# Small transfers on eight DMA engines, and the first output sums moved ahead of the last weight chunk

## The chip, the core and the metric

The kernel runs on one NeuronCore of a Trainium2 chip. The core has a matrix engine (PE, with its weight load PEld), a vector engine (DVE), a scalar engine (ACT), GpSimd (POOL) and a sync engine (SP). Sixteen DMA engines move data between the device memory (HBM) and the on-chip memory; in this kernel POOL issues the loads of inputs and weights, and SP issues constants, small copies and the output. The metric is the device time of one execution in microseconds, lower is better.

## The reference

Two stages run one after the other. The first is causal attention with a bias made from a running sum, for 8 batches, 8 heads, 576 tokens and 64 features per head. The second is a spectral mix over the result `x` of shape (8, 576, 512): the first 64 frequencies along the tokens are each multiplied by a complex 512 x 512 matrix of their own, transformed back, and the sum goes through one more product.

```python
# attention, per batch and head
cum = np.cumsum(np.maximum(s, 0.0), axis=-1)
scores = scale * (q @ k.T) + np.minimum(-(cum[:, None] - cum[None, :]), 0.0)   # causal
x = softmax(scores) @ v                       # heads side by side: (B, S, 512)
# spectral mix
X = np.fft.rfft(x, axis=1)[:, :64]
Y = zeros; Y[:, m] = X[:, m] @ (w_r[m] + 1j * w_i[m])       # 64 modes
y = np.fft.irfft(Y, n=S, axis=1)
u = x + y
out = u + np.maximum(u @ w_ch, 0.0)
```

The inputs `w_r` and `w_i` are 64 x 512 x 512 floats each, 134 MB together, and are by far the largest thing that is read.

## The kernel before

**Attention and forward transform.** A step `n` of 32 handles two heads of one batch: group `g` (four of them, 128 of the 512 features each) and batch `b`. POOL loads q, k and v. `transposes` turns q and k into `qt` and `kt`, `scores` forms the exponentials, `av` the weighted sums, which go to `x_all`; `fft` multiplies them with the transform matrix `Ff_sb` into `xs`. The row of running sums that the bias needs is row 64 of `qt`. For the first two steps `cum_rows` copies it from the on-chip tile `ncum_sb`. That tile is also stored once to device memory, `ncum_dram` (L586), and for the 30 later steps `cum_rows` loads two rows of it (L342), one for each head.

**Weights.** The 64 modes are cut into 8 chunks of 8 (`c`, `NCK` = 8). For each group, chunk and real or imaginary part the weights are one unit of 1 MB as bf16, read as float32 and converted on the way. POOL issues a unit as two transfers (the last one as four), in the order group, chunk, real, imaginary. `modes(g, c)` multiplies a chunk: 16 products in four groups of four, the first two groups with the real part, the last two with the imaginary part. A dictionary `meanwhile` can put other work ahead of one of the four groups (L486 to L494). Groups 0 to 2 add their products to `y_acc`; the last group (`g` = 3) gives, with `y_acc`, the finished `y_sb` of the chunk.

**Back transform and output.** The output has 4608 rows, made as 18 pairs of 128 rows (`pairs`). For pair `i`, `us[i]` is x plus the back transform of Y, and `zs[i]` is the same times `w_ch`. The back transform is a product of `G_sb` (128 rows, 16 for each chunk: 8 modes, real and imaginary) with `yv`. The tile `yv` holds the chunks' rows on its partitions, once as Y (`which` = 0) and once as Y times `w_ch` (`which` = 1). A chunk's 128 result rows (modes by batches) become 16 partitions by 8 batches by copies on chip: for the early chunks in `gather`, from chunk 4 on partly with a transfer on SP's queue, `spread` (L511 to L513): chunks 4 and 5 send `which` = 1, chunks 6 and 7 send both.

For the first two pairs the sums over chunks 6 and 7 do not wait for `spread`. `add_last` multiplies the chunk's result, as it stands, with a sparse copy of the matrix, `Gx_sb` (and `Gt_sb` for the 64 left-over tokens). These are loaded from the constants `d_Gx` and `d_Gt` (L634, L638). `add_y` with rows up to `GK` = 96 covers chunks 0 to 5.

The order around the end is written out by hand (L862 to L918): chunks 0 to 5, then chunk 6 with its transposes (`y_transposed`) and its product with `w_ch` (`y_times_wch`), then chunk 7 with two pieces of other work put inside. Ahead of chunk 7's third group stands `first_z` for both pairs: the z sums over chunks 0 to 5 (12 products for `add_y` and `add_last` together), and ahead of the fourth group `first_u`: x itself (`add_x`), the u sums over chunks 0 to 5, and chunk 6's share. After chunk 7 the last transposes, its product with `w_ch`, and a list of steps for all pairs, given as a string (L953), lead to the 20 output transfers on SP's queue.

**Constants.** `G_sb` is loaded from `d_G` with 128 rows (L280). Each DMA engine works off its share of a transfer as packets, one for each contiguous row, and ends it with a small packet that raises a semaphore.

Of the kernel before, what the change touches and what calls it, by code (L numbers as in the profile page):

```python
# [11 lines left out]
BF16 = mybir.dt.bfloat16  # L12
# [6 lines left out]
def kernel(  # L19
# [11 lines left out]
    nc = tc.nc  # L31
    B, H, S, D = q.shape
# [6 lines left out]
    NPAIR = B * H  # L39
    NG = DM // P  # L40
# [5 lines left out]
    MC = 8  # L46
    NCK = NM // MC
# [12 lines left out]
    HP = P // 2  # L60
# [25 lines left out]
        np.concatenate([negm_np, negm4_np], axis=1).astype(np.float32), name="c_negm"  # L86
    ).ap()
    d_Ff = nc.inline_tensor(Ff_np, name="c_Ffwd").ap()
    d_G = nc.inline_tensor(G_np, name="c_Ginv").ap()

    NX = 2
    Gx_np = np.stack([G_np[2 * MC * c :, : NF * P][: 2 * MC] for c in range(NCK - NX, NCK)], axis=1)
    d_Gx = nc.inline_tensor(np.ascontiguousarray(Gx_np), name="c_Ginvx").ap()
    Gt_np = np.stack([G_np[2 * MC * c :, NF * P : S][: 2 * MC] for c in range(NCK - NX, NCK)], axis=1)
    d_Gt = nc.inline_tensor(np.ascontiguousarray(Gt_np), name="c_Ginvt").ap()

    ctx.enter_context(tc.manual_schedule())
    gp = ctx.enter_context(tc.tile_pool(name="globals", bufs=1))
# [15 lines left out]
    auxpool = aux.enter_context(tc.tile_pool(name="aux_psum", bufs=2, space=PSUM, side="right"))  # L114

    dpool = ctx.enter_context(tc.tile_pool(name="dram", bufs=1, space=bass.MemoryType.DRAM))
    ncum_dram = dpool.tile([NPAIR, S + HP], BF16, name="ncum_dram")
    at = ExitStack()
    ap_ = at.enter_context(tc.tile_pool(name="attn", bufs=1))
    qkpool = at.enter_context(tc.tile_pool(name="qk_sb", bufs=2))  # L120
# [215 lines left out]
    def cum_rows(n):  # L336
        if n >= N:
            return
        g, b = divmod(n, B)
        p0 = b * H + 2 * g  # L340
        if n >= 2:
            nc.sync.dma_start(out=qt[n % NQ][D : D + 1, :, :], in_=ncum_dram[p0 : p0 + 2, :S].unsqueeze(0))  # L342
            return
        for h in range(2):
            nc.sync.dma_start(out=qt[n % NQ][D : D + 1, h, :], in_=ncum_sb[p0 + h : p0 + h + 1, :])
# [124 lines left out]
    def modes(g, c, meanwhile=None):  # L470


        ps = auxpool.tile([P, DM], FP32, name="yp", tag="aux")
        cols = xs[g % 2].rearrange("p q k h r b m -> p q k (h r b) m")

        def product(ri, q_, cg):
            k0 = HP if ri == 1 and c == 0 and cg == 0 else 0
            nc.tensor.matmul(  # L478
                ps[32 * cg : 32 * cg + 32, :],
                cols[k0:, q_, 1 - ri, :, c * MC // 2 + cg],  # L480
                wt[(g, c, ri)][cg // 2][k0:, 2 * (cg % 2) + q_, :],
                start=(ri == 0 and q_ == 0), stop=(ri == 1 and q_ == 1),
                tile_position=(k0, 32 * cg), skip_group_check=True,
            )

        for x in range(4):  # L486
            ri, y = divmod(x, 2)
            if meanwhile and x in meanwhile:
                meanwhile[x]()
            for z in range(4):  # L490
                if meanwhile:
                    product(ri, z // 2, 2 * y + z % 2)
                else:
                    product(ri, y, z)  # L494
        if g == 0:
            nc.vector.tensor_copy(out=y_acc[:, c, :], in_=ps)
        elif g < NG - 1:
            nc.vector.tensor_tensor(out=y_acc[:, c, :], in0=ps, in1=y_acc[:, c, :], op=ALU.add)  # L498
        else:
            yb = spool.tile([P, DM], FP16, name="y_sb", tag="y")  # L500
            for cols in halves if c == NCK - 1 else [slice(0, DM)]:
                nc.vector.tensor_tensor(
                    out=yb[:, cols], in0=ps[:, cols], in1=y_acc[:, c, cols], op=ALU.add
                )
            if c >= NCK - 2:
                spread(c, 0, yb)
            return yb
# [2 lines left out]

    def spread(c, which, rows):  # L511

        nc.sync.dma_start(out=yv[16 * c : 16 * c + 16, :, which, :], in_=rows)  # L513

# [65 lines left out]
    with tc.tile_pool(name="sc_psum", bufs=2, space=PSUM) as scpool, \  # L582
            tc.tile_pool(name="tr_psum", bufs=1, space=PSUM) as trpool, \
            tc.tile_pool(name="av_psum", bufs=1, space=PSUM) as avpool:
        cum_rows(0)
        nc.sync.dma_start(out=ncum_dram[:, :S], in_=ncum_sb)  # L586
        transposes(0, 0)
        transposes(0, 1)
        load(loads_qk(2) + loads_v(2))
        pad_p()  # L590
        for n in range(N):
            if n in (0, 2):
                nc.vector.memset(xs_flat[n // 2].bitcast(FP32), 0.0)
            tails_due = loads_tails(n // B + 1)[n % B - 3 : n % B - 2] if 2 < n % B < 5 else []
            load((loads_qk(n + LA) if n % 2 else []) + loads_v(n + LA) + tails_due, loads_w(on_chip[n]))
            if n == N // 2 + 1:
                nc.gpsimd.dma_start(out=wch_sb, in_=moe_w_ch.rearrange("(dt p) e -> p dt e", p=P))
            cum_rows(n + 1)
            scores(n, 0)
            av(n - 1, 1)  # L600
            if n and n % B == 0:
                scores(n, 1)
                fft(n - 1)
                av(n, 0)
                mode_products(n, 0)
                transposes(n + 1, 0)
                mode_products(n, 1)
                transposes(n + 1, 1)
                continue
            mode_products(n)  # L610
            transposes(n + 1, 0)
            scores(n, 1)
            i = first_pairs[n - N + len(first_pairs)] if n >= N - len(first_pairs) else None
            if i is not None:
                first_transposed(i, 0)
            transposes(n + 1, 1)
            fft(n - 1)
            av(n, 0)
            if i is not None:
                first_product(i, 0)  # L620
                first_transposed(i, 1)
            if i is not None:
                first_product(i, 1)
        av(N - 1, 1)
        fft(N - 1)
# [72 lines left out]
    def y_transposed(yb, c=NCK):  # L698
        ps = auxpool.tile([P, DT, P], FP16, name="yt_ps", tag="aux")
        for dt in range(DT):  # L700
            nc.tensor.transpose(ps[:, dt, :], yb[:, bass.ts(dt, P)], ident16h)
        yt = yt_first[:, :, c % NY, :] if c < NCK - 2 else spool.tile([P, DT, P], FP16, name="yt_sb", tag="yt")
        nc.scalar.copy(out=yt, in_=ps)
        return yt
# [104 lines left out]
    def u_of(i):  # L809
        return [us[i][:, x, :] for x in range(2)]  # L810
# [48 lines left out]
    def z_of(i):  # L859
        return [zs[i, x] for x in range(2)]  # L860
# [20 lines left out]
    assert not order_z and not ahead  # L881
    c = NCK - 2
    yb6 = modes(NG - 1, c)
    yt = y_transposed(yb6)
    vb6 = y_times_wch(c, yt)


    def first_u():
        add_x(0)
        add_y(u_of(0), 0, 0, slice(0, GK))  # L890
        add_last(u_of(0), 0, yb6, c=0)

    def first_z(i):
        add_y(z_of(i), i, 1, slice(0, GK))
        add_last(z_of(i), i, vb6, c=0)

    yb = modes(NG - 1, NCK - 1, {2: lambda: (first_z(0), first_z(1)), 3: first_u})

    yt = spool.tile([P, DT, P], FP16, name="yt_sb", tag="yt")
    for x in range(2):  # L900
# [95 lines left out]
```

## Time and profile before

| what | value |
|---|---|
| median of 3 runs | 441.92 us (440.32 to 442.31) |
| the profiled execution's own time | 442.11 us |
| its span, first to last instruction | 440.3 us |
| mean granted PE clock | 0.925 |
| busy: PE, DVE, ACT, POOL | 340.8, 252.5, 226.0, 171.7 us |
| read from HBM, written | 163.58 MB, 9.51 MB |
| share of the chain that ended last: DMA, PE, DVE | 53%, 25%, 15% |
| chunk 7's first products start | 399.35 us |
| chunk 7's last group of products starts | 406.48 us |
| first output transfer is issued | 411.97 us |

The chain of waits is made by going back from the last instruction, at each step to what released it. The span is what the profiler saw between the first and the last instruction; the time of a run includes some 1.8 us around it. Times inside the kernel are counted from the start of the span. The clock column of a window is the share of full speed that PE was granted: a product of 512 columns takes 0.22 us at full and 0.43 us at half clock.

### The profile page before, as it was taken

To read this page: it belongs to the slowest core of one execution; us is meant where nothing else is said; L and a number is where in the kernel's file an instruction comes from. 1 tells how busy PE (TensorE), PEld (TensorE's weight loads), DVE (VectorE), ACT (ScalarE), POOL (GpSimd) and SP (SyncE) were. 2 spreads that over 40 slices of the span, in tenths; PEclk is the share of its full clock that TensorE was granted. 3 is DMA by queue.
4 is the path that set the end of the run, shared out by engine and by line. 5 is a ranking of instruction groups with operands and counts; after the bars stand their busy time and mean duration, and the time that the engine had idled before them with its cause. 6 is when DMAs were issued, how large, how long until landed. Compare 5 with 4: busy or idle time off the path is not lost.

```text
span 440.3 us, 10592 instructions
## 1 busy us (share of the span) xinstructions
PE 340.8 (77%) x4409; PEld 203.7 (46%) x4409; DVE 252.5 (57%) x574; ACT 226.0 (51%) x421; POOL 171.7 (39%) x257
## 2 busy tenths in 40 slices
PE   1588999899695977973939458899987797778995
PEld 1365666465463644641616125556554345432341
DVE  7667776677573555752715315766655344450795
ACT  1387878267463634860727024766651334330794
POOL 6555454424353444323444343433322212310293
PEclk9999999999988888995968767999999989996999
DMA  9999999999999999999999999999999999996498
GB/s 179 207 206 206 204 206 208 207 209 207 207 205 207 210 207 210 207 209 208 205 209 208 209 208 209 207 210 206 210 211 212 212 211 211 203 218 121 155 381 347
DMA packets 69063, 93.30 MB, mean 212 GB/s; under 512 B 25932, under 2 KB 27592, under 8 KB 69016
## 3 DMA queue, kind: packets, MB, share of 16 engines
q0 software_dynamic: 61424, 81.28, 104.6%
q1 hardware_dynamic: 7592, 11.36, 7.2%
q8 instruction: 34, 0.56, 0.5%
q14 instruction: 13, 0.11, 0.1%
HBM read 163.58 MB, written 9.51 MB: 393 GB/s over the span
## 4 chain that ended last, share of the span: by engine, by line
DMA 53%; PE 25%; DVE 15%; issue 3%; POOL 2%; ACT 1%; DVEq 0%; POOLq 0%
DMA w_sb<-in_moe_w_i_dram 21%; DMA w_sb<-in_moe_w_r_dram 17%; DMA qk<-in_k_dram 8%; DMA qk<-in_q_dram 5%; PE sc_ps L397 3%; DVE xs L468 3%; DVE qt L359 3%; PE z_ps L681 3%; PE yp L478 3%; DVE x_all L443 2%; PE av_ps L433 2%; PE sc_ps L391 2%; PE tr_ps L355 2%; DVE xt L553 2%; PE z_ps L773 2%
## 5 line engine op out<-in xcount | busy, mean ns | idle before, releaser
L405 ACT ACTIVATE p_sb<-sc_ps,cumt_sb 128x576 f16<-128x576 f32 (+1 forms) x256 | 141.9, 636 | 21.8 <-PE sc_ps L397 21.4
L397 PE MATMUL sc_ps<-qt,kt 128*128 128x512 bf16 (+2 forms) x384 | 76.8, 312 | 6.9 <-ACT kt L359 6.1
L243 POOL DMA_DIRECT2D v<-in_v_dram x72 | 51.4, 714 | 60.6 <-DMA w_sb<-in_moe_w_i_dram 12.8
L243 POOL DMA_DIRECT2D w_sb<-in_moe_w_i_dram x62 | 38.5, 623 | 89.2 <-DMA w_sb<-in_moe_w_i_dram 28.3
L359 DVE COPY qt<-tr_ps 64x576 bf16<-64x576 bf16 x64 | 47.8, 747 | 41.5 <-PE tr_ps L355 41.5
L478 PE MATMUL yp<-w_sb,xs 128*32 128x512 bf16 (+1 forms) x480 | 42.2, 431 | 29.1 <-DMA w_sb<-in_moe_w_i_dram 25.4
L355 PE MATMUL tr_ps<-ident,qk 64*64 64x64 bf16 x1152 | 34.3, 205 | 33.8 <-DMA qk<-in_k_dram 16.0
L243 POOL DMA_DIRECT2D w_sb<-in_moe_w_r_dram x60 | 37.4, 624 | 53.0 <-DMA w_sb<-in_moe_w_r_dram 33.3
L397 PEld LDWEIGHTS <-kt 128*128 128x128 bf16 x384 | 38.3, 105 | 34.5 <-ACT kt L359 12.8
L391 PE MATMUL sc_ps<-negm,ident 128*128 128x256 bf16 x256 | 53.5, 293 | 0.1
L355 PEld LDWEIGHTS <-qk 64*64 64x64 bf16 x1152 | 26.4, 117 | 51.7 <-DVE kt L359 20.3
L376 ACT ACTIVATE p<-sc_ps,cumt 128x64 f16<-128x64 f32 x32 | 10.1, 314 | 73.8 <-PE sc_ps L372 73.6
L433 PE MATMUL av_ps<-v,p_sb 128*128 128x65 f16 x1024 | 44.2, 197 | 1.8 <-DVE x_all L443 0.6
L359 ACT COPY kt<-tr_ps 64x576 bf16<-64x576 bf16 x32 | 22.8, 714 | 40.8 <-DVE qt L359 40.1
L433 PEld LDWEIGHTS <-p_sb 128*128 128x128 f16 x1024 | 37.4, 100 | 9.6 <-DVE x_all L443 5.4
L468 DVE CAST xs<-ft_ps 64x128 bf16<-64x128 f32 x128 | 36.7, 287 | 7.3 <-PE ft_ps L458 5.7
L478 PEld LDWEIGHTS <-xs 128*32 128x32 bf16 (+1 forms) x512 | 17.8, 146 | 46.0 <-DMA w_sb<-in_moe_w_i_dram 24.6
L438 DVE TENSOR_REDUCE den<-av_ps 128x5 f32<-128x10 f32 x64 | 10.8, 169 | 48.3 <-PE av_ps L433 47.3
L443 DVE TENSOR_TENSOR x_all<-av_ps,rcp 128x320 f16<-128x320 f32 x64 | 31.5, 492 | 2.2
L498 DVE TENSOR_TENSOR y_acc<-yp,y_acc 128x512 f32<-128x512 f32 x16 | 11.1, 692 | 29.2 <-PE yp L478 28.5
L539 ACT COPY z<-z_ps 128x512 f32<-128x512 f32 x22 | 12.9, 586 | 26.9 <-PE z_ps L571 14.2
L458 PE MATMUL ft_ps<-Ff_sb,x_all 128*64 128x192 f16 (+1 forms) x320 | 24.4, 266 | 1.0 <-DVE x_all L443 1.0
(107 smaller groups left out, 439.4 us busy)
## 6 DMA issues: line engine op xcount, KB each, us to landing
w_sb<-in_moe_w_r_dram POOLq DMA_DIRECT2D x60, 512.0 KB, 13.6
w_sb<-in_moe_w_i_dram POOLq DMA_DIRECT2D x55, 512.0 KB, 13.2
out_dram<-r_w SPq DMA_DIRECT2D x16, 512.0 KB
v<-in_v_dram POOLq DMA_DIRECT2D x72, 64.0 KB, 11.1
qk<-in_q_dram POOLq DMA_DIRECT2D x15, 288.0 KB, 12.0
qk<-in_k_dram POOLq DMA_DIRECT2D x15, 288.0 KB, 13.2
x_all<-in_moe_w_r_dram POOLq DMA_DIRECT2D x4, 512.0 KB, 8.4
w_sb<-in_moe_w_i_dram POOLq DMA_DIRECT2D x3, 384.0 KB, 12.7
```

Source lines behind the costliest of these rows:

```text
L243: nc.gpsimd.dma_start(out=dst, in_=src)
L355: nc.tensor.transpose(ps[rows, r, :], src[rows, r, :], ident16[rows, rows])
L359: copy(out=to[:, :, :, half * RH : half * RH + RH], in_=ps[HP * i : HP * i + HP].rearrange("d r (h p) -> d h p r", h=2),)
L391: nc.tensor.matmul(ps[:, bass.ds(w * S, W)], ident16, negm[:, bass.ts(r, W)], start=True, stop=False, skip_group_check=True,)
L397: nc.tensor.matmul(ps[:, c0 : c0 + i1 - i0], keys[:, w, r, :], qh[:, i0:i1], start=False, stop=True, skip_group_check=True,)
L405: nc.scalar.activation(out=pt[:, poff[x] : poff[x] + S - w * W], in_=ps[:, w * S : (w + 1) * S - w * W], func=ACTF.Exp, bias=cumt_sb[:, x, ...
L433: nc.tensor.matmul(ps[:, I, r : r + NCH], lhsT, rhs, start=(i == 0), stop=(i == len(todo) - 1), skip_group_check=True,)
L443: nc.vector.tensor_tensor(out=x_all[:, g, b, :, D * h : D * h + D], in0=ps[:, :, 1 : NCH], in1=rcp.unsqueeze(2).to_broadcast([P, NT, D]), ...
L458: nc.tensor.matmul(ps[HP * q_ : HP * q_ + HP].rearrange("p h f -> p (h f)"), x_all[:nT, g, b, T, q_::2], Ff_sb[:nT, T, :], start=(T == 0), ...
L468: nc.vector.tensor_copy(out=xs[g % 2][HP * h : HP * h + HP, q_, :, h, :, b, :], in_=a)
L478: nc.tensor.matmul(ps[32 * cg : 32 * cg + 32, :], cols[k0:, q_, 1 - ri, :, c * MC // 2 + cg], wt[(g, c, ri)][cg // 2][k0:, 2 * (cg % 2) + ...
L681: nc.tensor.matmul(zs[i, x], xts[i][:, x, dt, :], wch_sb[:, dt, :], start=(dt == 0), stop=(last and dt == DT - 1), skip_group_check=True,)
```

## The change

The change has two parts. It has no effect on what is computed.

The first part lays out small transfers on SP's queue so that the outermost dimension of one side has eight entries. The constants `G_sb`, `Gx_sb` and `Gt_sb` are read from an array of eight blocks with an unused row behind each. The running sums are stored in pieces of 144 values, with 16 unused values between, and a step's two rows are read as eight pieces of 288 bytes where before there were two of 1152. `spread` sends a chunk's 16 rows as two transfers of eight rows; chunk 7 keeps one transfer of 16.

The second part moves work of the first two pairs. `add_x`, the u sums over chunks 0 to 5 and chunk 6's u share go from inside chunk 7 to around chunk 6's transposes. The z sums over chunks 0 to 5 go to behind chunk 6's product with `w_ch`, ahead of all of chunk 7's products. Chunk 6's z share (`add_last` with `vb6`) stays ahead of chunk 7's third group.

```diff
+    def eighths(a, name):
+        n = len(a) // 8
+        t = np.zeros((8, n + 1) + a.shape[1:], a.dtype)
+        t[:, :n] = a.reshape((8, n) + a.shape[1:])
+        return nc.inline_tensor(t, name=name).ap()[:, :n]
-    d_G = nc.inline_tensor(G_np, name="c_Ginv").ap()
+    d_G = eighths(G_np, "c_Ginv")
-    d_Gx = nc.inline_tensor(np.ascontiguousarray(Gx_np), name="c_Ginvx").ap()
+    d_Gx = eighths(Gx_np, "c_Ginvx")
-    d_Gt = nc.inline_tensor(np.ascontiguousarray(Gt_np), name="c_Ginvt").ap()
+    d_Gt = eighths(Gt_np, "c_Ginvt")
...
-    ncum_dram = dpool.tile([NPAIR, S + HP], BF16, name="ncum_dram")
+    NE8 = 8
+    CP = 2 * S // NE8
+    ncum_dram = dpool.tile([NPAIR, S // CP, CP + 16], BF16, name="ncum_dram")
...
-            nc.sync.dma_start(out=qt[n % NQ][D : D + 1, :, :], in_=ncum_dram[p0 : p0 + 2, :S].unsqueeze(0))
+            nc.sync.dma_start(
+                out=qt[n % NQ][D : D + 1, :, :],
+                in_=ncum_dram[p0 : p0 + 2, :, :CP].rearrange("h x t -> (h x) t"),
+            )
...
     def spread(c, which, rows):
-        nc.sync.dma_start(out=yv[16 * c : 16 * c + 16, :, which, :], in_=rows)
+        n = 2 * MC if c == NCK - 1 else NE8
+        for r in range(0, 2 * MC, n):
+            nc.sync.dma_start(
+                out=yv[2 * MC * c + r : 2 * MC * c + r + n, :, which, :], in_=rows[B * r : B * (r + n), :]
+            )
...
-        nc.sync.dma_start(out=ncum_dram[:, :S], in_=ncum_sb)
+        nc.sync.dma_start(
+            out=ncum_dram[:, :, :CP], in_=ncum_sb.rearrange("c (x t) -> c x t", t=CP)
+        )
...
     yb6 = modes(NG - 1, c)
+    add_x(0)
     yt = y_transposed(yb6)
+    add_y(u_of(0), 0, 0, slice(0, GK))
+    add_last(u_of(0), 0, yb6, c=0)
     vb6 = y_times_wch(c, yt)
-
-    def first_u():
-        add_x(0)
-        add_y(u_of(0), 0, 0, slice(0, GK))
-        add_last(u_of(0), 0, yb6, c=0)
+    add_y(z_of(0), 0, 1, slice(0, GK))
+    add_y(z_of(1), 1, 1, slice(0, GK))
     def first_z(i):
-        add_y(z_of(i), i, 1, slice(0, GK))
         add_last(z_of(i), i, vb6, c=0)
-    yb = modes(NG - 1, NCK - 1, {2: lambda: (first_z(0), first_z(1)), 3: first_u})
+    yb = modes(NG - 1, NCK - 1, {2: lambda: (first_z(0), first_z(1))})
```

## The prediction

> **What bounds the kernel now.** I read the slices first, then the chain of waits from 335 us on, then the clock by stretches, last the transfers and their completion marks. The slices show DMA busy at nine tenths or more up to slice 36 at a steady 203 to 218 GB/s after the first slice: until about 405 us the weight stream sets the pace. The chain says how that hands over to the tail (columns: start, length, what):
>
> ```profile
> 335.86 16.85 DMA w_sb<-in_moe_w_i_dram
> ...
> 352.75 0.66 PE yp L478 x7
> ...
> 381.76 0.45 POOL w_sb L243
> ...
> 383.57 15.64 DMA w_sb<-in_moe_w_r_dram
> ...
> 399.35 1.09 PE yp L478 x6
> 400.44 0.96 PE z_ps L773 x2
> 401.41 0.85 PE z_ps L784 x2
> 402.26 0.99 PE z_ps L773 x3
> 403.25 0.85 PE z_ps L784 x3
> 404.11 1.00 PE yp L478 x4
> 405.11 0.57 PE u_ps L803 x2
> 405.68 0.43 PE u_ps L773 x2
> 406.12 0.43 PE u_ps L784 x2
> 406.55 0.60 PE yp L478 x4
> ```
>
> A weight load that lands at 352.71 starts chunk 3's products; from there PE work leads to the issue of the last loads at 381.76; chunk 7's real weights land at 399.21. From 399.35 the chain is PE alone: two groups of products, the sums of the first two pairs (L773, L784), a group, the u sums, the last group. By the timeline that group starts at 406.48. Its weights were there at 405.13 (below), so PE is 1.35 us late. Everything after it (33.9 us: last transposes, 18 result pairs, 9.4 MB out) hangs on that start, and the output queue is full from 419.6 on (402 GB/s), so I shift the tail one to one.
>
> Why PE is late shows in the windows (from:to, length, PE busy, PEld, DVE, ACT, POOL, granted clock, DMA share, GB/s), cut at the steps in which the clock changes in this trace, 3.41 us:
>
> ```profile
> 394.91:398.33 3.42, 1.43 (x8) 0.53 (x8) 1.09 (x2) 0.59 (x1) 0.00 (x0) 1.00 1.12 215
> 398.33:401.74 3.41, 2.39 (x12) 0.68 (x12) 0.00 (x0) 0.00 (x0) 0.00 (x0) 0.50 1.01 201
> 401.74:405.15 3.41, 3.41 (x15) 0.85 (x14) 0.00 (x0) 0.00 (x0) 0.00 (x0) 0.50 0.32 67
> 405.15:408.57 3.42, 2.85 (x17) 1.07 (x17) 0.76 (x2) 0.59 (x2) 0.00 (x0) 1.00 0.00 0
> ```
>
> A window with PE busy for 1.43 us is followed by half clock; a full window restores it. In the other such steps 1.50 us or less was followed by half clock and 1.85 or more never.
>
> The transfers (the first line: packets, MB, share; then KB each):
>
> ```profile
> q8 instruction: 34, 0.56, 0.5%
> ...
> yv<-v_sb SPq DMA_DIRECT2D x4, 128.0 KB
> ...
> qt<-ncum_dram SPq DMA_DIRECT2D x30, 2.2 KB
> ```
>
> The trace keeps a completion mark per DMA engine, sixteen a load. For the weight load issued at 367.91 six fall at 382.87 to 384.10, two at 385.31 and 385.43, eight at 386.59 to 387.48; this stagger grows from 1 us at 20 us and then stays. The packets explain it. The 34 instruction packets take 0.89 to 1.39 us each, and their durations repeat with a period of eight: eight engines in turn, about four packets each, 4 x 0.94 = 3.8 us, the lag of the late eight. Each of the 30 qt loads has two outermost rows and shows two packets of 1152 B, 64 ns plus a 22 ns mark: 30 x 86 ns = 2.58 us on two engines, the two of the early half that lie 2.5 behind. So the end the row count starts from lies in the early half.
>
> **The change part by part.**
>
> *Layout.* Two rows gave two engines, so I read eight outermost rows as eight engines from the same end: the early half. A late engine loses G_sb 8 x 64 + 22 = 534 ns, Gx 96 + 22, Gt 4 x (31 + 22) = 212 (together 0.86 us by 345 us), and four spreads at 8 x 59 + 22 = 494 ns, 1.98 us. Its last mark goes from 405.13 to 402.3. An early engine gains G 0.51, Gx 0.10, Gt 0.12, and 30 qt packets of 288 B. That size is not in the trace: 384 B took 22 ns, 256 B 18 to 41, so with its mark 40 to 63 ns, 1.2 to 1.9 us in all; I take 1.3 (the 384 B row is by far the most frequent). The two former qt engines lose as much. The ncum_dram store stays on sixteen, 16 packets for 4 on each: under 0.2 us, long before it is read.
>
> The latest of the six: 384.10 + 0.73 + 1.3 = 386.1. Then eight loads, 4 x 2.47 + 4 x 1.24 = 14.84 us (check: a late engine took 387.4 to 404.17 = 16.8, which is 14.84 and the four spreads), plus three doubled spreads, 2.97, gives 403.9; of the fourth, chunk 6's v, a third gets in before the end: 404.2. Bounds: 403.4 (cheap packets, early marks) and 405.6 (dear packets, all of the fourth spread). So the late and the early half nearly change places and the last weights land 0.9 us earlier, not 2.8. The landing at 352.71 moves by up to 0.86, and with it PE's stretch to 381.76; that keeps the early engines fed and is inside the sum.
>
> *Sums.* Out of chunk 7 go add_x (0.57), the u sums (0.43 + 0.43) and the z sums over G (0.96 + 0.99): 3.4 us as the clock was. The six z products over Gx stay. After: two groups from 399.35 at most (0.65 to 1.09), z over Gx (0.87 to 1.7), a group (0.45 to 1.0): PE is ready by 403.2 even at half clock, so the last group waits for its weights and starts at 404.2 + 0.1 = 404.3 instead of 406.48: -2.2 us. Had the layout done nothing it would be 405.23, -1.25.
>
> In their new place: add_x (0.43) fits the 0.80 us in which PE waits for y_sb (L701). Four u products, 0.87, cover the 0.68 wait for the ACT copy and delay v_ps by 0.2. Six z products (0.9) wait for chunk 5's v spread, and chunk 7's products stand behind them on PE. It was issued at 390.07 and landed at 396.42; as two transfers it has eight more packets per engine, each turn 155 ns of weights (2.47 us / 16) and 59 of its own: 1.7 us later, 398.1. The sums end at 399.1, when the weights land anyway. If that slips, 403.2 to 404.3 is 1.1 us of cover; beyond it each us counts. On SP each spread becomes two issues of 0.55: y6 and v6 queue behind the earlier halves, v6 ends near 405.5, needed first by U1 about 409. Nothing of POOL moves.
>
> *Clock.* The row speaks against this change. It takes work out of a stretch in which PE waits for DMA: between about 400 and 404.3 only one group (0.45) and the rest of the z products remain, so some 3.41 us step there holds under 1.4 us, and half clock follows, now behind the last group instead of before it. Price at half clock: last group 0.42 (1.07 against 0.65), transposes 0.1, u product 0.43, v products 0.45, second half of v and z about 0.8: 2.2, and with X1 and U1 (0.62 each) 3.4. Low end 0, where the step falls so that the slow time ends in the wait. I take 0.95, a drop that ends about 407 and catches the first three.
>
> The Trainium skill ("TensorE: Matmul & The Clock Gate", Part 1) states that the clock halves after an idle window of about 3.4 us, and that the window runs free of the kernel. Read strictly, with a wholly idle window needed, this term would be 0 and the time 439.7; this trace halves the clock at 1.43 us busy, so the measurement decides and the term stays.
>
> Sum: -2.2 + 0.95 = -1.25 us on the profiled 442.11 (span 440.3 and 1.8 around it), which stands 0.2 above the median 441.92: 440.7.
>
> **Rivals.**
> *The halves balance and the clock holds.* If qt's packets cost little and the fourth spread comes after the weights, they land near 403.1; the last group starts at 403.2, PE's own bound, -3.3 us: 438.6. For it: the work merely moves and the mean of the last marks is 402.6. Against: the 1.43 row.
> *The drop catches the whole opening.* Steps with 2.39 and 2.48 us busy stayed at half clock, so it may last 6.8 us: +3.4. With weights at 404.2 that is +1.2, 443.1; with 405.2, +2.2, 444.1, slower than before. It decides from a loss over 2.2 us on. For it: nothing fills PE's wait.
> *The named eight are the late ones, or get too much.* Then the last mark is 405.13 + 1.98 + 0.73 + 1.3 = 409.1, +2.7 us: 444.6. It decides from a last mark after 406.4. Against: the two qt engines lie with the early ones; but that all eight do is inferred.
> *It does nothing.* At full clock PE would have been ready for the old last group at about 404.2, so the sums were hidden behind 405.13 anyway, and the layout gives back what it takes: 441.9.
>
> **How the numbers follow.** Forecast 0.40 (440.7, own range 439.2 to 442.2), balance 0.28, whole opening 0.14, wrong eight 0.14, nothing 0.04. A measurement of this kernel tells about 0.5%, 2.2 us: the borders are 439.7 and 444.1. Faster: all of balance and 0.14 of the forecast, 0.42. Slower: the wrong eight and 0.10 of the opening, 0.24. Same: 0.34. The range reaches down past balance, 438.0, and up to 443.8; the wrong eight and the worst of the opening lie outside.
>
> **What would show it.** Marks: all sixteen of the last load within about 2.5 us, the last near 404.2; spreads in pairs of 64 packets. The timeline: L803 and L773 before 399, the last L478 group idle on DMA w_i until then. The windows: half clock after 404 rather than 398 to 405. I am wrong if the last mark is after 405.2, if z over G ends after 400.5, or if the opening (last group to first output, 5.5 us before) is unchanged.

## The result and the profile after

The changed kernel is slower: 446.01 us median of 6 runs (444.53 to 447.24) against 441.24 (440.32 to 442.31) for the kernel before beside it, a ratio of 1.0102 with a 95% interval of 1.0085 to 1.012. The forecast was 440.7 us, a gain of 1.2 us, with 443.8 as the upper end of its range: the sign was wrong, and the change costs 4.8 us. The profiled execution took 446.47 us with a span of 444.7, 4.4 more than the 440.3 of before, at a mean granted clock of 0.89 against 0.925.

The chain of waits of the changed kernel, from the last weights on (start, length, what):

```profile
389.19 18.91 DMA w_sb<-in_moe_w_i_dram
408.10 0.04 issue
408.14 1.09 PE yp L490 x4
...
409.25 0.44 DVE y_sb L514
...
409.74 0.73 PE yt_ps L920 x4
410.46 0.85 PE u_ps L802 x2
411.31 1.71 PE v_ps L927 x8
413.02 2.10 PE z_ps L802 x11
```

Before, the chain came to the last group through PE's own work. Now it comes through the last weight transfer, whose last mark falls at 408.10 instead of 405.13. The last group starts at 408.14, 1.66 us later than the 406.48 of before. And the steps that follow have become dearer: in the chain the z products (z_ps) take 2.10 us, and by the timeline eight v products (v_ps) take 1.91. The same two steps before, from the timeline and from the chain:

```profile
408.54 1.04 PE L911 MATMUL v_ps<-wch_sb,yt_sb 128*128 128x256 f16 x8
```

```profile
409.65 1.38 PE z_ps L784 x12
```

The timeline of PE in the same stretch (start, length, line, operation, tiles; in brackets the idle time before and who ended it):

```profile
399.90 1.16 PE L791 MATMUL z_ps<-yv,G_sb 96*128 96x512 f16 x6 [1.51 <-DMA yv<-v_sb]
402.00 1.08 PE L490 MATMUL yp<-w_sb,xs 128*32 128x512 bf16 x8 [0.95 <-DMA w_sb<-in_moe_w_r_dram]
...
405.64 1.07 PE L490 MATMUL yp<-w_sb,xs 128*32 128x512 bf16 x4 [0.60 <-DMA w_sb<-in_moe_w_i_dram]
408.14 1.07 PE L490 MATMUL yp<-w_sb,xs 128*32 128x512 bf16 x4 [1.43 <-DMA w_sb<-in_moe_w_i_dram]
```

PE waits four times for a transfer between 398 and 408. The windows show what that does to the clock (from:to, length, PE busy, PEld, DVE, ACT, POOL, granted clock, DMA share, GB/s):

```profile
397.96:401.37 3.41, 1.58 (x8) 0.26 (x6) 0.69 (x1) 0.00 (x0) 0.00 (x0) 1.00 1.09 192
401.37:404.79 3.42, 2.79 (x14) 0.55 (x14) 0.00 (x0) 0.00 (x0) 0.00 (x0) 0.50 0.63 114
404.79:408.20 3.41, 1.38 (x8) 0.25 (x8) 0.00 (x0) 0.00 (x0) 0.00 (x0) 0.50 0.14 29
408.20:411.61 3.41, 2.88 (x13) 1.13 (x14) 0.76 (x2) 0.70 (x2) 0.00 (x0) 0.50 0.07 19
411.61:415.03 3.42, 3.42 (x19) 1.48 (x17) 0.87 (x3) 0.65 (x2) 0.00 (x0) 0.50 0.15 40
```

A window with 1.58 us busy is followed by half clock, which stays through windows with 2.79, 1.38 and 2.88 us busy and through one that is busy throughout. The opening, from the last group to the first output's issue at 415.73, runs at half but for its last 0.7 us: it takes 7.59 us, 5.49 before.

The transfers (a queue's packets, MB and share; then issues and KB each):

```profile
q8 instruction: 34, 0.56, 0.5%
...
qt<-ncum_dram SPq DMA_DIRECT2D x30, 2.2 KB
...
yv<-v_sb SPq DMA_DIRECT2D x6, 64.0 KB
```

As many instruction packets as before; the spreads go in halves of 64 KB. The sixteen marks of the last weight load are at 400.36 to 405.16 for thirteen engines, then 405.95, and two by themselves at 408.01 and 408.10. The load was issued 1.42 us later than before, but that is not what makes it late: thirteen engines end by 405.16, where all sixteen of before ended by 405.13, and only the last two end 3 us behind that.

So the 4.4 us of span are 1.66 (last group later) + 2.10 (opening) + 0.64 (first output to the end: 28.97 us, 28.33 before).

### The profile page after: what moved, and what is told of

Its sections match the earlier page's. It is cut to its first block, busy times and chain, and to the rows that moved or that the text cites. A ratio compares the mean times of both kernels' runs of the same rounds, so it can differ in the third digit from the quotient of the medians.

```text
span 444.7 us, 10602 instructions
## 1 busy us (share of the span) xinstructions
PE 350.3 (79%) x4409; PEld 207.3 (47%) x4409; DVE 253.0 (57%) x574; ACT 226.4 (51%) x421; POOL 171.6 (39%) x257
## 4 chain that ended last, share of the span: by engine, by line
DMA 57%; PE 22%; DVE 12%; issue 4%; POOL 2%; ACT 1%; DVEq 0%; POOLq 0%
DMA w_sb<-in_moe_w_r_dram 35%; DMA w_sb<-in_moe_w_i_dram 14%; DMA v<-in_v_dram 3%; PE yp L490 3%; PE sc_ps L409 3%; PE av_ps L445 3%; DMA qk<-in_q_dram 3%; DVE qt L371 3%; DMA qk<-in_k_dram 2%; DVE xs L480 2%; PE sc_ps L403 2%; DVE x_all L455 2%; PE tr_ps L367 2%; DVE kt L371 1%; PE u_ps L821 1%
## 5 line engine op out<-in xcount | busy, mean ns | idle before, releaser
L409 PE MATMUL sc_ps<-qt,kt 128*128 128x512 bf16 (+2 forms) x384 | 80.1, 322 | 6.2 <-ACT kt L371 5.3
L490 PE MATMUL yp<-w_sb,xs 128*32 128x512 bf16 (+1 forms) x480 | 43.3, 439 | 26.6 <-DMA w_sb<-in_moe_w_i_dram 24.1
L409 PEld LDWEIGHTS <-kt 128*128 128x128 bf16 x384 | 39.3, 108 | 35.8 <-ACT kt L371 12.2
L403 PE MATMUL sc_ps<-negm,ident 128*128 128x256 bf16 x256 | 55.1, 301 | 0.0
L371 DVE COPY kt<-tr_ps 64x576 bf16<-64x576 bf16 x32 | 24.4, 763 | 0.4
```

What stands on the lines that cost most here:

```text
L371: copy(out=to[:, :, :, half * RH : half * RH + RH], in_=ps[HP * i : HP * i + HP].rearrange("d r (h p) -> d h p r", h=2),)
L403: nc.tensor.matmul(ps[:, bass.ds(w * S, W)], ident16, negm[:, bass.ts(r, W)], start=True, stop=False, skip_group_check=True,)
L409: nc.tensor.matmul(ps[:, c0 : c0 + i1 - i0], keys[:, w, r, :], qh[:, i0:i1], start=False, stop=True, skip_group_check=True,)
L490: nc.tensor.matmul(ps[32 * cg : 32 * cg + 32, :], cols[k0:, q_, 1 - ri, :, c * MC // 2 + cg], wt[(g, c, ri)][cg // 2][k0:, 2 * (cg % 2) + ...
```

## The experiments

The theory after the result: the eight engines of an eight-row transfer and the engines that serve instruction packets have some members in common (three of them, by the first reading), these get both loads, and the last weights wait for them; and moving the sums away leaves PE too little to do in its wait, so the clock is halved through the opening. All runs, with the last mark, the start of the last group and the issue of the first output from each profile (us):

| run | median (runs) | ratio, 95% interval | last mark | last group | first output |
|---|---|---|---|---|---|
| before | 441.24 (6) | 1 | 405.13 | 406.48 | 411.97 |
| changed | 446.01 (6) | 1.0102 [1.0085, 1.012] | 408.10 | 408.14 | 415.73 |
| sums_only | 442.72 (12) | 1.0011 [0.9995, 1.0027] | 406.12 | 406.16 | 413.34 |
| layout_only | 444.51 (4) | 1.0056 [1.0038, 1.0074] | 408.39 | 408.43 | 413.92 |
| filled | 444.84 (4) | 1.0057 [1.0041, 1.0073] | 407.20 | 407.24 | 412.73 |
| z_ahead | 441.06 (7) | 0.9971 [0.9957, 0.9985] | 405.42 | 405.47 | 410.95 |
| u_ahead | 442.08 (10) | 1.0012 [0.9999, 1.0024] | 404.63 | 404.68 | 411.16 |
| rows8 | 441.81 (10) | 1.0008 [0.9995, 1.0022] | 405.67 | 406.19 | 411.68 |
| spread8 | 443.17 (10) | 1.0034 [1.0022, 1.0046] | 405.80 | 407.17 | 412.65 |
| rows6, rows4, consts8 | 441.5, 441.63, 441.7 (one each) | | 405.23, 405.11, 404.56 | 405.83, 405.97, 406.04 | 411.31, 411.46, 411.54 |
| late_spread | 444.05 (12) | 1.0044 [1.0025, 1.0063] | 404.05 | 404.10 | 409.59 |
| v6_late | 441.74 (12) | 1.0006 [0.9989, 1.0022] | 405.30 | 405.34 | 410.83 |
| extra8, extra4 | 452.07, 449.95 (one each) | | | | |
| even8, even6, even4 | 443.36, 443.93, 441.86 (one each) | | | | |

Each ratio is against runs of the kernel before on the same chip; their medians there were 442.25 (sums_only, layout_only, filled, z_ahead), 441.27 (rows, spread8), 441.61 (late_spread, u_ahead, consts8) and 441.36 (v6_late); 441.23 stood beside extra8 and extra4, and 442.34 beside the three runs named even. The last mark alone scatters: with the old transfers it lies anywhere from 404.63 to 406.12. Marks, starts and windows are those of one profiled execution of each kernel; that of `sums_only` (443.5 us) was near the top of its runs, that of `u_ahead` (441.31) the fastest of its ten.

### The two halves of the change, each alone

`sums_only` keeps all transfers of before and takes the changed order of the sums:

```diff
     yb6 = modes(NG - 1, c)
+    add_x(0)
     yt = y_transposed(yb6)
+    add_y(u_of(0), 0, 0, slice(0, GK))
+    add_last(u_of(0), 0, yb6, c=0)
     vb6 = y_times_wch(c, yt)
+    add_y(z_of(0), 0, 1, slice(0, GK))
+    add_y(z_of(1), 1, 1, slice(0, GK))
...
-    yb = modes(NG - 1, NCK - 1, {2: lambda: (first_z(0), first_z(1)), 3: first_u})
+    yb = modes(NG - 1, NCK - 1, {2: lambda: (first_z(0), first_z(1))})
```

> The changed order of the sums with the transfers as before. Theory (last weights are late through the eight-engine layout alone, and PE's idling before them halves the clock behind them): last weight mark near 405.1 as before, last group of products starts at 405.25 (1.2 us earlier), but the clock is half in the opening and first output comes 7.6 us after that start instead of 5.5: about 442.1 us, some 0.9 over before. Rival (the moved sums themselves cost, through their wait for chunk 5's v transfer): chunk 7's first products start after 400.5 and the time is 444 or more.

Its windows (columns as above) and its last group in PE's timeline:

```profile
400.96:404.37 3.41, 1.58 (x10) 0.33 (x8) 0.00 (x0) 0.00 (x0) 0.00 (x0) 1.00 0.55 93
404.37:407.78 3.41, 1.09 (x5) 0.22 (x6) 0.50 (x2) 0.00 (x0) 0.00 (x0) 0.50 0.04 8
407.78:411.19 3.41, 3.41 (x16) 1.96 (x16) 0.79 (x3) 0.71 (x2) 0.00 (x0) 0.50 0.16 43
```

```profile
406.16 1.07 PE L478 MATMUL yp<-w_sb,xs 128*32 128x512 bf16 x4 [2.02 <-DMA w_sb<-in_moe_w_i_dram]
```

PE is ready 2.02 us before the weights, and pays with the clock: 7.18 us from there to the first output. The move alone takes PE off the path and gives the time back in the opening; there is no gain that can be measured. The rival, that the moved sums cost through their wait for chunk 5's v, is out: chunk 7's first products start at 400.14.

`layout_only` is the other half: the changed kernel with the sums where they were.

```diff
     yb6 = modes(NG - 1, c)
-    add_x(0)
     yt = y_transposed(yb6)
-    add_y(u_of(0), 0, 0, slice(0, GK))
-    add_last(u_of(0), 0, yb6, c=0)
     vb6 = y_times_wch(c, yt)
-    add_y(z_of(0), 0, 1, slice(0, GK))
-    add_y(z_of(1), 1, 1, slice(0, GK))
```

> The eight-engine layout with the sums where they were. Theory: last weight mark near 408.1, three marks apart from the others by 1 us or more, last group starts at 408.2 (1.7 us later than before); the sums inside chunk 7 keep PE busier, so the opening takes 5.5 to 6.5 us: 443 to 444 us. Rival (the layout alone does nothing, all comes from the order of the sums): last mark 405, 441.2 us.

```profile
408.43 0.65 PE L490 MATMUL yp<-w_sb,xs 128*32 128x512 bf16 x4 [0.60 <-DMA w_sb<-in_moe_w_i_dram]
```

The same late weights (marks 405.82, 407.65 and 408.39; the other thirteen by 403.63), but the group's four products take 0.65 us, full clock, because the sums keep PE busy until 407.8. The opening is 5.49. So the layout makes the weights late, and the sums' place decides the clock. In the profiles the halves nearly add up: the layout alone starts the last group 1.95 us later and leaves the opening as it was, the sums alone start it 0.32 us sooner and lengthen the opening by 1.69; together it is 1.66 and 2.10.

### Work put into the wait

`filled` is the changed kernel with 18 products that nobody reads, placed where PE waits.

```diff
     vb6 = y_times_wch(c, yt)
+    fill_ps = auxpool.tile([P, DM], FP32, name="fill_ps", tag="aux")
+    def fill(n):
+        for _ in range(n):
+            nc.tensor.matmul(fill_ps, ident16h, wch_sb[:, 0, :], start=True, stop=True, skip_group_check=True)
+    fill(4)
...
-    yb = modes(NG - 1, NCK - 1, {2: lambda: (first_z(0), first_z(1))})
+    yb = modes(NG - 1, NCK - 1, {2: lambda: (first_z(0), first_z(1), fill(6)), 3: lambda: fill(8)})
```

> The changed kernel with 18 products more on PE, into a tile that nothing reads, put into its waits: 4 ahead of the z sums, 6 and 8 ahead of chunk 7's third and fourth group. Theory: weights land as in the changed kernel (408.1), but the clock stays whole and the opening takes 5.5 us instead of 7.6: 2 us under the changed kernel, 443.9 us. Rival (the opening is longer because of late copies or the output queue, not the clock): 446 or more, opening 7.6.

```profile
402.55 1.47 PE L911 MATMUL fill_ps<-wch_sb,ident16h 128*128 128x512 f16 x6
404.20 0.65 PE L490 MATMUL yp<-w_sb,xs 128*32 128x512 bf16 x4 [0.19 <-DMA w_sb<-in_moe_w_i_dram]
404.79 1.90 PE L911 MATMUL fill_ps<-wch_sb,ident16h 128*128 128x512 f16 x8
407.24 0.65 PE L490 MATMUL yp<-w_sb,xs 128*32 128x512 bf16 x4 [0.56 <-DMA w_sb<-in_moe_w_i_dram]
```

Useless work keeps the clock: no half-clock window from 383 to 437 us, and the opening is 5.49 us instead of 7.59. The time falls from 1.0102 to 1.0057 of before, that of layout_only. Not all of the gain arrives: from the first output to the end this execution takes 30.07 us, 28.97 in the changed kernel. It shows 35 instruction packets instead of 34, the last at 432.80 (0.96 us), amid the output. That the packet costs the microsecond wasn't tried by itself.

### Only one of the sums moved

`z_ahead` has the transfers of before and moves the z sums over `G_sb` alone; `u_ahead` moves `add_x` and the u sums alone.

```diff
 (z_ahead)
     vb6 = y_times_wch(c, yt)
+    add_y(z_of(0), 0, 1, slice(0, GK))
+    add_y(z_of(1), 1, 1, slice(0, GK))
...
-        add_y(z_of(i), i, 1, slice(0, GK))
         add_last(z_of(i), i, vb6, c=0)
...
 (u_ahead)
     yb6 = modes(NG - 1, c)
+    add_x(0)
     yt = y_transposed(yb6)
+    add_y(u_of(0), 0, 0, slice(0, GK))
+    add_last(u_of(0), 0, yb6, c=0)
...
-    yb = modes(NG - 1, NCK - 1, {2: lambda: (first_z(0), first_z(1)), 3: first_u})
+    yb = modes(NG - 1, NCK - 1, {2: lambda: (first_z(0), first_z(1))})
```

> Transfers as before; only the z sums over chunks 0 to 5 are moved ahead of chunk 7, the u sums stay inside it. Theory: PE has 2 us less to do after 399.35 and still no long wait, so the last group starts when its weights are there, 405.25, and the clock is whole again by the opening (5.5 us): 440.0 us, 1.2 under before. Rival (the clock halves in the opening as it does with all sums moved): 442.

> The transfers of before; add_x, the u sums over chunks 0 to 5 and chunk 6's u share moved to around chunk 6's transposes, the z sums left inside chunk 7. If what costs the opening its clock is the amount of PE work that is left between chunk 7's real weights and its last ones, this stretch now holds the z sums alone: PE is ready before 405, the last group starts at about 405.3 with the weights, and the opening is 5.5 us where the windows stay above 1.6 us busy, up to 7 us where one falls below: 440.0 to 441.5. Rival: the u sums are what mattered in the move (they stand directly ahead of the last group), so moving them alone gives no less than the full move, 442.7.

The last group of `z_ahead`, and two windows of `u_ahead`:

```profile
405.47 0.65 PE L478 MATMUL yp<-w_sb,xs 128*32 128x512 bf16 x4 [0.25 <-DMA w_sb<-in_moe_w_i_dram]
```

```profile
401.88:405.29 3.41, 1.26 (x8) 0.39 (x8) 0.00 (x0) 0.00 (x0) 0.00 (x0) 1.00 0.25 55
405.29:408.70 3.41, 2.88 (x15) 1.68 (x14) 1.13 (x3) 0.70 (x2) 0.00 (x0) 0.50 0.16 43
```

With the u sums left as filling, PE comes to the last group 0.25 us before its weights, at full clock: opening 5.48, and 0.9971 of before. That is 0.3%, less than the 0.5% that the prediction took as the border, but with seven runs the interval leaves 1 out. By this one comparison it beats both kernels. With the u sums moved instead, PE waits 1.98 us, the window holds 1.26 us, and the opening is 6.48: no gain. Expected were 440.0 to 441.5 us; the rival was right, for 1.0012 is what the full move gives (1.0011). That the u sums are the better filling because they stand directly ahead of the last group fits both runs, but was not tried apart from their amount.

### Which part of the layout, and which engines

`rows8`, `rows6` and `rows4` change only the running sums, to eight, six or four pieces; `spread8` only `spread` for chunks 4 to 6; `consts8` only the constants.

```diff
 (rows8, with 6 or 4 for the others)
+    CP = 2 * S // 8
+    ncum_dram = dpool.tile([NPAIR, S // CP, CP + 16], BF16, name="ncum_dram")
...
+                in_=ncum_dram[p0 : p0 + 2, :, :CP].rearrange("h x t -> (h x) t"),
...
 (spread8)
+        n = 2 * MC if c == NCK - 1 else 8
+        for r in range(0, 2 * MC, n):
...
 (consts8)
+    d_G = eighths(G_np, "c_Ginv")
```

> Only the rows of running sums (qt) are read as eight pieces of 288 B, all else as before. Theory (three of the eight engines that an eight-row transfer uses also fetch the instruction packets): by 300 us three marks of a load stand about 1.4 us (29 x 54 ns) behind where the last ones stood before, 5 to 6.5 us after the first; the last weight mark moves from 405.1 to about 406.5, little more than the 406.5 at which PE is ready: 442 to 443 us. Rival (all eight are early engines, and only the whole load together makes them late): the last marks stay with the engines of before, less than 5 us after the first, last weight mark 405.1, 442 us.

> The same rows in six pieces of 384 B, so six engines. Theory, if the engines that fetch instructions are the upper ones of the eight: fewer late marks than with eight pieces, one instead of three. Rival (they lie at the bottom, or all six are free): three, or none.

> The same rows in four pieces of 576 B, so four engines, with more time on each (30 x some 65 ns = 2.0 us) than with eight. Theory (overlap with the instruction engines, upper ones of the eight): no mark is later than before, stagger at 300 us below 5 us, last weight mark 405.1. Rival (it is the load put on few engines that delays, whichever they are): marks 2 us behind, more than with eight pieces.

> Only the spreads of chunks 4 to 6 go as two transfers of eight rows each, all else as before. Theory (three engines serve instructions and spreads): stagger at 300 us as before (under 5 us), then the late engines of the eight get 4 x 0.49 = 2.0 us more and the others 2.0 us less: last weight mark 407, two or three marks 2 us or more behind the rest, last group at 407.1: 442.9 us. Rival (the eight are the early engines): last weight mark 403.5, last group still PE-bound at 406.5: 442.2 us.

> Only the constants G_sb, Gx_sb and Gt_sb in eight blocks; rows, spreads and order of before. If the loads add up on the engines that they overlap, these gain 0.73 us: 404.17 becomes 404.9, still ahead of the 405.1 of the last engine, and the time is that of before (441.5 to 442.5). Rival: the constants make most of the 3 us by which the layout moved the last mark: last mark about 407, time 443.5.

No part alone makes the weights 3 us late. For `rows8` a last mark of about 406.5 was expected and 405.67 came; for `spread8` 407 was expected and 405.80 came. The spreads cost most, 0.34% (interval 0.22% to 0.46%), and through another wait than expected, so that it was luck that the expected 442.9 us nearly came (443.17): chunk 7's first products start at 400.23 after 2.74 us of waiting (399.35 before) and run at half clock, so that PE itself comes to the last group 1.4 us after its weights. Rows and constants alone cost nothing that shows. For the marks this fits an addition on the same engines: before, the instruction half ended at 404.17, but for one engine at 405.13. (From the 33rd instruction packet on, at 390.25 us, one mark of each load stands 0.5 to 2 us behind the rest: by count, the engine that serves a fifth packet.) So rows (1.62), spreads (1.98) or constants (0.73) alone bring the others to 404.9 to 406.2, about the scatter of the last mark, while all three bring them to 408.5. These runs could not tell which engines have both loads: the marks' lag scatters as much as rows of four or eight differ.

Two further runs put one transfer of eight or four rows of 8 KB (322 ns each) beside each step's rows, in the kernel before:

```diff
+    extra_src = nc.inline_tensor(np.zeros((8, 4160), np.float16), name="c_extra").ap()
+    extra = dpool.tile([8, 32, 4160], FP16, name="extra")
...
+            nc.sync.dma_start(out=extra[:, n, :4096], in_=extra_src[:, :4096])
```

> The kernel before, with one more transfer for each of the 30 later steps: eight rows of 8 KB each from a constant to an unused array in device memory, so that the engines that an eight-row transfer uses fall far behind and the sixteen marks of a weight load fall apart into groups: neither, instruction packets alone (about 3.8 us), eight rows alone, both. Theory: some of the eight also carry instruction packets, so the marks show a group of two or three that lie about 3 to 4 us behind the other six or five of the eight, and as many fewer in the group of instructions alone. Prediction's reading, as rival: the eight are all without instruction packets, and there are two groups of eight.

> The same with four rows of 8 KB for each step. If the first four of the eight carry no instruction packets (the four-piece rows showed no added delay), four marks lie behind in one group and none of them by a further 3 to 4 us, and all the engines of the instruction group are still there. Rival: one or two of the four lie 3 to 4 us behind the others of the four.

With four rows, four marks stand 4.23 to 6.34 us behind the first for the weight load issued at 344.36 us and the other twelve within 1.24: no one of the four is 3 us behind the rest. With eight rows there were no clean groups (at 345.90 seven within 1.11 us, then 1.40 to 6.71 without a wide gap until the last two): too much load for a clear answer, and the two-row loads that this kernel keeps load two of the engines more. So the last three runs load all engines of the transfer alike and by about as much as the instruction packets do: the rows in eight, six or four pieces, and beside them as many rows of 1 KB (59 ns).

```diff
 (even8: rows8, and)
+    extra_src = nc.inline_tensor(np.zeros((8, 640), np.float16), name="c_extra").ap()
+    extra = dpool.tile([8, 32, 640], FP16, name="extra")
...
+            nc.sync.dma_start(out=extra[:, n, :512], in_=extra_src[:, :512])
```

> Rows of running sums in eight pieces and beside them eight rows of 1 KB for each step, so that every engine of the eight gains the same: 54 ns and about 81, 30 times, 4.0 us, about as much as an engine of the instruction half (3.8 us at the end, about 3 at 300 us). Theory: two to three marks of a weight load at 300 us lie 6 to 7 us behind the first, as many engines carry neither and stand in front, the ten to twelve others lie between. Prediction's reading, as rival: eight disjoint engines, so that all sixteen marks lie within 1.5 us of each other at 300 us.

> The same with six pieces and six rows. If the engines that carry both are the last two of the eight, no mark stands apart at the back: the latest are within 1 us of the next ones at 300 us. If they are the fifth and sixth, two marks lie 3 us behind the others as with eight.

> The same with four pieces and four rows. Expected: four and eight engines with a like load, four in front, none at the back by itself. If the first four carry instruction packets, one mark or more lies 3 us behind the others.

The sixteen marks of the weight load issued nearest to 345 us, in us behind the first of them:

| run | in front | between | apart at the back |
|---|---|---|---|
| even8 | 0, 0.20 | twelve, 2.23 to 4.51 | 6.51, 6.73 |
| even6 | 0, 0.26, 0.94 | twelve, 2.37 to 5.24 | 6.73 |
| even4 | 0, 0.01, 0.14, 0.38 | twelve, 3.62 to 5.25 | none |

The counts fit one picture. With eight engines that serve instructions and k engines of a k-row transfer of which j are common to both, 16 - 8 - k + j engines have neither load and j have both. Four rows: j = 0, four in front. Six: j = 1, three in front, one at the back. Eight: j = 2, two in front, two at the back. (For six rows no mark at the back or two had been expected; one came.) If the rows are always dealt out from the same engine on, an eight-row transfer uses six engines of the early half and two of the late one; the first four are all early, one of the two common ones comes in with the fifth or sixth row and one with the seventh or eighth. The picture stands on one execution of each run, but each gives the same j twice, in front and at the back.

The kernels with the whole layout show the two as well. In `filled` the load issued at 346.65 has two marks in front (0 and 0.25), twelve between (1.95 to 4.76) and two at the back (6.43 and 6.52); in the changed kernel and `layout_only` the marks at that time form no clean groups. And the second half of chunk 6's v, the last transfer of eight rows, has one mark 1.0 us after its issue and then eight more. Six of these fall by 406.32 in the changed kernel (406.70 in `layout_only`, 405.06 in `filled`) and two at 407.56 and 407.90 (408.36 and 408.80; 406.85 and 406.96), within 0.8 us of the two late marks of the weights in each. By these times the two engines that hold up the weights are two of the eight of an eight-row transfer, and the other six do not hold them up. That the instruction packets are what these two carry besides is the reading of the counts; the trace does not name engines. What sets the third mark back (405.95, 405.82 in `layout_only`) is open.

### Two attempts to go further

Both start from `z_ahead`, and take spreads of chunk 6 out of the way of the last weights: `late_spread` sends y and v of chunk 6 behind chunk 7's y, `v6_late` only v.

```diff
-            if c >= NCK - 2:
+            if c == NCK - 1:
                 spread(c, 0, yb)
...
-        spread(c, 1, vb)
+        if c < NCK - 2:
+            spread(c, 1, vb)
...
     yb = modes(NG - 1, NCK - 1, {2: lambda: (first_z(0), first_z(1)), 3: first_u})
+    spread(c, 0, yb6)
+    spread(c, 1, vb6)
```

> The transfers of before with only the z sums moved ahead (the version that took 0.9971 of before), and chunk 6's two spreads issued on SP behind chunk 7's instead of ahead of the last weights. If a transfer in front of the last weights costs a late engine its own packets (494 ns each), the last mark goes from 405.4 to about 404.4; PE has then to come through the two z shares, so the last group starts at about 405.2 and the opening stays 5.5 us: first output 410.7 to 411.0, about 440.8. Rival: the late spreads land after 411 and U1 or the second pair's z product waits for them: first output 412 or later, 442 or more.

> The version with the z sums ahead, and only chunk 6's v spread issued behind chunk 7's y spread; the y spread stays ahead of the last weights. If the late spreads cost only by U1's wait for the y6 rows, that wait is gone: last mark near 404.6, last group at about 405.0 (PE's own work bounds it), first output 410.5, third at 413.2, 440.6 to 441. The v6 rows land near 410.5 and are needed at 411.5. Rival: any spread behind the last weights comes too late for the second pair's z product, also v6's: the third output is issued after 413.6 and the time is 442 or more.

The chain of waits of `late_spread`, and one line of PE's timeline of `v6_late`:

```profile
406.16 4.77 DMA yv<-y_sb
410.93 0.04 issue
410.98 0.62 PE u_ps L774 x4
```

```profile
411.77 0.39 PE L774 MATMUL z_ps<-yv,G_sb 112*128 112x512 f16 x1 [0.78 <-DMA yv<-v_sb]
```

`late_spread` issues its first output at 409.59, the earliest of all, and then U1, the u sums of the second pair, waits 1.78 us for the y6 rows. That is the wait that the rival named, though behind the first output and not ahead of it; its 442 us or more came true. Fifteen marks of that spread fall by 409.81, the sixteenth at 410.93; an instruction packet of 1.28 us had started at 407.27, while the spread was under way. In `v6_late` the v6 rows land by 410.62 but for one mark at 411.73 (an instruction packet of 1.44 us had started at 408.76), and the second pair's z waits 0.78 for it. Its rival was right in the mechanism, not in the time (442 or more): the third output is issued at 414.27, 413.55 in `z_ahead`, and the median is 441.74. Of `late_spread`'s median of 444.05 its profile shows little, for the profiled execution took 441.56, near the low end of its runs (441.2 to 445.11). What the others lose is open.

## Why the prediction was wrong, point by point

- **The eight engines: the step that failed.** "Two rows gave two engines, so I read eight outermost rows as eight engines from the same end: the early half." The text itself called it inferred, and the sum was built on it all the same. Two engines of the eight serve instruction packets too, as the three runs with even loads count and as the marks of the last spread bear out. The prediction's own rows give their load: 404.17 + 0.73 + 1.62 + 1.98 = 408.5, measured 408.01 and 408.10 and, in layout_only, 407.65 and 408.39; predicted 404.2 with 403.4 to 405.6 as bounds. The bounds were made from prices alone and left the place out, which only a rival with 0.14 held. Of the 5.6 us between the forecast for the profiled execution (442.11 - 1.25 = 440.86) and its 446.47, this step makes 3.8 (last group at 408.14, 404.3 predicted), the clock 1.15, the tail 0.6.
- **The price of a 288-byte packet.** Within its bounds: 32 ns and a mark of 22, 30 times 1.62 us, where 1.3 was taken.
- **The sums.** The last group waits for its weights, as said. Of the 2.2 us sooner that was said, 1.25 were the sums' share; sums_only starts that group 0.3 us sooner than before, with a last mark that fell late (406.12), z_ahead 1.0. "It does nothing" was wrong in reason as well: PE's work did hold up the last group.
- **The z sums over G** slipped as feared: the second half of chunk 5's v spread landed at 399.85, not 398.1, and the six products started at 399.90. It cost nothing on the path, since chunk 7's weights let PE wait 0.95 us more until 402.00. But the 1.51 us of wait ahead of it lie in the window that held 1.58 us of work, the one that was followed by half clock.
- **The clock.** The drop was foreseen and mis-sized: 0.95 us taken, +2.10 measured, against the 2.2 priced for a whole opening. filled and layout_only show the cause: the same transfers with PE busy give 5.49 us. The trace had the row that decides it, half clock that survived windows with 2.39 and 2.48 us busy; in the changed kernel 2.79 and 2.88 did not release it either.
- **The skill's rule on the clock.** The Trainium skill ("TensorE: Matmul & The Clock Gate", Part 1) ties the slow clock to an idle window; here 1.58 us of work in a window of 3.41 was not enough to keep the clock, so leaning on the measured row was right.
- **The rivals.** Two slower ones came together. "The named eight are the late ones, or get too much" said a last mark of 409.1, measured 408.10; "the drop catches the whole opening" said how the rest went. They were weighed as alternatives with 0.14 each, but neither excludes the other: layout_only shows the late weights with the clock whole in the opening, sums_only the slow opening with the transfers of before. The two priced together, 2.7 + 2.2 on 441.9, are 446.8, against 446.01 measured; no case in the sum held that.
- **The earlier landing at 352.71** did not come: the last transfer was issued at 389.19, 387.77 before. The tail was shifted one to one but for 0.64 us.

## What to carry to other kernels

When a load is moved among DMA engines, count from a run which engines are meant, with a probe that loads all of them alike: marks in groups say how many have neither, one or both loads, and the slowest engine, not the mean, sets the landing. Work that is moved out of a wait takes the clock along: look at the busy time of the windows ahead of the critical group, move what PE cannot hide, and leave enough there to keep it busy (here the u sums, with only the z sums moved, gave the best version). Rivals that do not exclude each other are to be priced together, not only side by side.

## What the runs showed of the hardware that was not expected

- By the counts above (inferred, one execution of each) a six-row transfer shares one DMA engine with the instruction packets, an eight-row one two, a four-row one none.
- Around chunk 7 every window of 3.41 us with at most 1.58 us of PE work that is quoted here was followed by half clock. There is no sharp border in the busy time. In u_ahead a window with 1.85 us, at 330 us, was followed by half clock too, which the prediction had put on the safe side, and in the changed kernel one with 2.04, at 118 us. The way back has none either: 2.88 us busy at half clock did not bring the full clock back in the changed kernel (from 408.20), and did in u_ahead (from 405.29).
- In late_spread and v6_late one mark of a small transfer came 1.1 us behind the other fifteen, and with it the whole transfer, while an instruction packet of 1.3 to 1.4 us ran or had just run. That the packet held it up is inferred.
- With 18 more products (filled) the trace has one more instruction packet, in the middle of the output.
